# Full-array state reads, and the row of scores fetched through DRAM, in a cross-attention block followed by a mixture-of-depths layer

## The chip, the cores and the metric

One core of one Trainium2 chip. The metric is device time in microseconds of one execution; the kernel before has a median of 221.9 us over 3 runs (221.47 to 222.27). Less is better. Engines are called by their profile names: PE is TensorE's matmul, PEld its weight load, DVE VectorE, ACT ScalarE, POOL GpSimd, SP the engine whose queue issues most DMAs.

## What is computed

There are 8 batches. Each has 8 heads of 512 tokens x 64 values (x) and 8 heads of 32 state rows x 64 values (state), all f32. An attention block reads in both directions, and its 512 + 32 = 544 rows of 512 values go through a layer that only the 128 rows with the highest gate score pass:

```python
scores = scale * np.matmul(x, state.transpose(0, 1, 3, 2))      # per head 512 x 32
a = softmax over the 32 state rows;   xread = np.matmul(a, state)
scores2 = scale * np.matmul(state, x.transpose(0, 1, 3, 2))     # per head 32 x 512
a2 = softmax over the 512 tokens;     sread = np.matmul(a2, x)
x = concatenate([xread, sread]) with heads side by side         # 8 x 544 x 512
scores = np.einsum('bsd,d->bs', x, w_gate)
out = x.copy()
for b in range(B):
    top_idx = np.argpartition(-scores[b], capacity)[:capacity]  # capacity 128
    xe = x[b, top_idx]
    ye = np.maximum(xe @ w1, 0.0) @ w2                          # w1 512 x 1024, w2 1024 x 512
    out[b, top_idx] = xe + sigmoid(scores[b, top_idx])[:, None] * ye
```

## The kernel before, in words

**Attention, per batch.** Tokens are cut into NC = 4 chunks of 128 rows. The heads are turned in pairs on TensorE (L340) and copied out to xT (L349, a ring of 12 buffers). One set of small matmuls makes the scores of all heads (L369) in a PSUM tile ps_s, from which both softmaxes are made. The token side is turned 32x32 by VectorE into e (L383), then max, subtraction, exp (ACT), sum, division, and turned back into eT (L405), a chain on VectorE of some 1.2 us per step. The state side takes its max on VectorE (L411) and its exp on ACT (L415), is turned on TensorE (L469), copied to aT (L472) and multiplied with x (L485), which gives the state rows xt (L490).

**Reads.** eT holds, for a chunk c and a group g of four heads, 4 x 32 = 128 rows: one per head and state row. The reads (L447) multiply it with st_v, which holds the state rows of two heads side by side with zeros elsewhere, and as a last column each state row's product with w_gate. Each matmul takes half the array (64 rows, 129 columns out), so a chunk takes four, written to one PSUM tile ps_o of two banks (a ring of 1). ACT copies the 512 values of a row to xs (L451), and VectorE sums the gate columns (4 per row) into sc[:, b, c] (L455). When the four chunks are there, xs is stored to the output by one DMA of 1 MB on SP (L512), the state rows by four small ones (L517). GpSimd fills st_v (`pool_states`, L223): a clear (L224) and four copies (L218), for batches 0 and 1, then for 2 to 7.

**Choice, per batch.** A row's place in the order of scores is found by counting. The 544 scores of a batch are laid as a row over all partitions (srow): TensorE turns each column of sc, broadcast, into ps_tr (L558 for the tokens, L561 for the state rows) and ACT copies the two pieces (L564, L567). VectorE compares srow with each chunk's column in five win instructions (L577) that also count; TensorE sums the wins (L604); VectorE makes offsets (L610, L611) and one-hots, one instruction per chunk (L617); TensorE picks the chosen rows' numbers and scores with them (L632); VectorE makes indices (L637); GpSimd fetches the chosen rows from the output by an indirect DMA (L524), which waits for the stores of the batch.

**Layer.** Batches go in the groups 0; 1, 2; 3, 4; 5, 6; 7. The fetched rows are turned (L690), multiplied with w1 (L707, 256 columns for two batches, 128 for one), taken through ReLU by ACT (L711), multiplied with w2 (L724), added to the fetched rows by VectorE (L727) and put back by an indirect DMA (L524).

**Order.** Every step is a `Piece` with an engine, a planned length, what must come before it and the ring buffers that it takes or uses. `carry_out` (L112) makes a list plan at build time: it takes the engine that is free first, and among the pieces that are ready within SOON of that engine's free time the one with the lowest key, which is the batch's or group's number plus the number in LATER for the piece's name. The order that comes out is fixed for each engine, and each engine runs its list in order, SP's DMA issues included.

Of the kernel before, what the change touches and what calls it, by code (L numbers as in the profile page):

```python
# [8 lines left out]
F32 = mybir.dt.float32  # L9
# [9 lines left out]
def kernel(  # L19
# [10 lines left out]
    nc = tc.nc  # L30
# [24 lines left out]
    def pool(name, bufs, **kw):  # L55
        return ctx.enter_context(tc.tile_pool(name=name, bufs=bufs, **kw))

    N_X, N_XR = 5, 8
# [4 lines left out]
    psum = pool("psum", 1, space=bass.MemoryType.PSUM)  # L63

# [5 lines left out]
    SOON = {"PE": 0.0000, "DVE": 0.4931, "ACT": 0.0000, "POOL": 1.8045, "SP": 0.3000}  # L70

    LATER = {
        "add": -100.0000, "below": 1.9500, "exp": -0.0600, "exps": -0.7084, "fetch": 0.2600, "first": 100.0000,
        "gate": -0.5600, "gate_s": 4.8280, "heads": 0.4872, "in": -1.0433, "index": -2.8646, "load": -50.0000,
        "load_x": -2.0000, "max": 4.0896, "mult": 4.3959, "numbers": 0.2545, "off": -1.9260, "oh": -2.4538,
        "out": 3.4200, "over": -2.2366, "parts": -2.6851, "pick": 0.3200, "put": -100.0000, "read": 4.9387,
        "relu": -100.0000, "row": -4.7962, "row_kept": 4.8694, "row_s": -3.1695, "row_s_kept": -0.1742,
        "rows": 5.0000, "score_s": -3.7680, "scores": -1.0816, "second": 100.0000, "sexp": -0.1370,
        "sigmoid": 0.2238, "smax": 1.1888, "sread": 1.2957, "srows": -2.7199, "ssum": 1.4281, "state_T": 0.3300,
        "state_gates": 2.6509, "states": -1.3434, "store": 4.7700, "sub": -1.8119, "sum": -4.7918,  # L80
        "tables": -4.6345, "turn": -0.1899, "turn_a": 4.0218, "turned": 4.7352, "turned_a": -5.0000,
        "twice": -2.9080, "win": 4.2491, "xg": 90.0000, "xg_kept": -100.0000,
# [29 lines left out]
    def carry_out():  # L112
# [7 lines left out]
        while left:  # L120
# [15 lines left out]
            assert ready, "the plan cannot go on"  # L136
# [19 lines left out]
    P_O = Ring("ps_o", [128, 1024], F32, 1, psum)  # L156
    P_H = Ring("ps_h", [128, 512], F32, 2, psum)
    R_X = Ring("xf", [128, H, NC, D], F32, N_X, xin)
    R_XT = sbuf("xT", [128, 2, 2, 128], 12)
# [4 lines left out]
    R_XS = sbuf("xs", [128, NC, Dm], 2)  # L164
# [32 lines left out]
    st_v = const.tile([128, B, 2, 2 * D + 1], F32, name="st_v")  # L197
# [8 lines left out]
    st_T = const.tile([128, B, 2, 128], F32, name="st_T")  # L206
    z0 = const.tile([128, 1], F32, name="z0")
# [5 lines left out]
    def state_V(lo, hi):  # L213

        for q in range(4):
            k = q % 2
            r = slice(Ns * q, Ns * (q + 1))
            nc.gpsimd.tensor_copy(out=st_v[r, lo:hi, :, D * k:D * (k + 1)], in_=st_c[r, lo:hi, :, 0])  # L218
# [8 lines left out]
    def state_gates(lo, hi):  # L227
        t = work.tile([128, hi - lo, 2, D], F32, name="state_g", tag="hT", bufs=1)
        nc.vector.tensor_tensor(out=t, in0=st_c[:, lo:hi, :, 0],
                                in1=wg_s.unsqueeze(1).to_broadcast([128, hi - lo, 2, D]), op=ALU.mult)  # L230
        nc.vector.reduce_sum(out=st_v[:, lo:hi, :, 2 * D], in_=t, axis=AX.X)

    def pool_tables():

        nc.gpsimd.iota(num[:, 0, :, 0:NC], pattern=[[SP, B], [1, NC]], base=0, channel_multiplier=NC)
        nc.gpsimd.iota(num[:, 0, :, NC], pattern=[[SP, B]], base=S, channel_multiplier=1)
        nc.gpsimd.iota(after, pattern=[[1, SP]], base=0, channel_multiplier=-1, allow_small_or_imprecise_dtypes=True)
        nc.gpsimd.tensor_scalar(after, after, 0.0, None, op0=ALU.is_gt)

        nc.gpsimd.iota(places, pattern=[[-128, NC + 1], [1, n_slots]], base=0, channel_multiplier=-1,  # L240
                       allow_small_or_imprecise_dtypes=True)
        nc.gpsimd.memset(ones, 1.0)


        nc.gpsimd.memset(sc, 0.0)

# [79 lines left out]
    def attention(b):  # L326
# [6 lines left out]
        for pair in range(H // 2):  # L333
# [18 lines left out]
            p = add("PE", 0.47 if b else 0.9, turn, after=[px[(pair * len(px)) // (H // 2)]] + last_turn[-1:], takes=[ps], uses=[xf[b]],  # L352
                    key=key("turn"))
            last_turn.append(p)
            p_xT.append(add(on, 0.6, keep, after=[p], takes=[t], uses=[ps], key=key("turned")))
# [17 lines left out]
        p_s = add("PE", 1.02, scores, after=p_xT + [p_sT[b]], takes=[s], uses=xT, key=key("scores"))  # L373
# [62 lines left out]
        p_xs, p_sc = [], []  # L436
        for c in range(NC):
            o = Buf(P_O)

            def view(o):  # L440
                return o.ap.rearrange("p (i g m) -> p i g m", i=2, g=2)

            def read(c=c, o=o):
                for g in range(2):
                    for i in range(2):
                        half = slice(D * i, D * (i + 1))
                        nc.tensor.matmul(view(o)[:, i, g, 0:2 * D + 1], eT.ap[half, c % 2, g, c // 2], st_v[half, b, g],  # L447
                                         start=True, stop=True)

            def keep(c=c, o=o):  # L450
                nc.scalar.copy(out=xs.ap[:, c].rearrange("p (g i m) -> p g i m", g=2, i=2),  # L451
                               in_=view(o)[:, :, :, 0:2 * D].rearrange("p i g m -> p g i m"))

            def gate(c=c, o=o):
                nc.vector.tensor_reduce(out=sc[:, b, c:c + 1], in_=view(o)[:, :, :, 2 * D], axis=AX.XY, op=ALU.add)  # L455

            p = add("PE", 0.66, read, after=[p_eT, p_pool[b], p_sg[b]], takes=[o], uses=[eT],
                    key=key("read"))
            p_sc.append(add("DVE", 0.15, gate, after=[p, p_tab], uses=[o], key=key("gate")))
            p_xs.append(add("ACT", 0.6, keep, after=[p], takes=[] if c else [xs], uses=[o] + ([xs] if c else []), key=key("rows")))  # L460

        aT, p_aT = [], []
        for g in range(2):
# [10 lines left out]
            p = add("PE", 0.5, turn, after=[p_a[g]], takes=[ps, t], uses=[a], key=key("turn_a"))  # L474
# [35 lines left out]
    def store_base(b, xs, tmp, p_xs, p_xt):  # L510
        def x_rows():
            touches(b, nc.sync.dma_start(out=out[b, 0:S].rearrange("(p c) m -> p c m", c=NC), in_=xs.ap))  # L512
# [16 lines left out]
    def choice(b, tmp, p_sc, p_xt, p_st1):  # L529
# [30 lines left out]
        def row_s():  # L560
            nc.tensor.transpose(ps2.ap[:, 0:Ns], sc[0:Ns, b, NC:NC + 1].to_broadcast([Ns, 128]), ident[0:Ns, 0:Ns])  # L561

        p = add("PE", 0.55, row_x, after=p_sc, takes=[ps1], key=key("row"))
        p_r1 = add("ACT", 0.59, lambda: nc.scalar.copy(out=srow.ap[:, 0:S], in_=ps1.ap), after=[p], takes=[srow],  # L564
                   uses=[ps1], key=key("row_kept"))
        p = add("PE", 0.2, row_s, after=[p_ss, p], takes=[ps2], key=key("row_s"))
        p_r2 = add("ACT", 0.2, lambda: nc.scalar.copy(out=srow.ap[:, S:SP], in_=ps2.ap[:, 0:Ns]), after=[p, p_r1],  # L567
                   uses=[srow, ps2], key=key("row_s_kept"))
# [38 lines left out]
        def offsets():  # L607
            off = tmp["off"] = small.tile([128, NC + 1], F32, name="off")
# [5 lines left out]
        def one_hot():  # L614
            for c in range(NC + 1):
                m = rows[c]
                nc.vector.tensor_scalar(oh.ap[0:m, c], places[0:m, c], tmp["off"][0:m, c:c + 1], None, op0=ALU.is_equal)  # L617
# [3 lines left out]
        p_oh = add("DVE", 1.06 * n_slots / 128, one_hot, after=[p], takes=[oh], key=key("oh"))  # L621
# [169 lines left out]
```

## Time and profile before

The page comes from one profiled execution. Its own time is 222.47 us: a span of 220.7 us on the core, and 1.8 us around it. The runs without it have their median at 221.9.

| | before |
|---|---|
| median of 3 runs | 221.9 us |
| the profiled execution | 222.47 us |
| its span | 220.7 us |
| first matmul starts | 4.07 us |
| last matmul ends | 215.4 us |
| PE busy, share of the span | 202.4 us, 92% |
| DVE, ACT, POOL busy | 124.5, 85.9, 49.9 us |
| granted TensorE clock | 0.999 |
| DMA | 26.59 MB in 17,406 packets |

How to read it: a group's line has line number, engine, operation, out<-in with shapes and count, then the busy time of the group in us and the mean length of one in ns, then the idle time of the engine ahead of it with what ended it. An f32 matmul has two records, so 128 matmuls are "x256". Matmuls overlap, so lengths of single records do not add up to time; the distance from one start to the next does. The view of windows gives the busy time of each engine between two times.

### The profile page before, as it was taken

To read this page: it belongs to the slowest core of one execution; us is meant where nothing else is said; L and a number is where in the kernel's file an instruction comes from. 1 tells how busy PE (TensorE), PEld (TensorE's weight loads), DVE (VectorE), ACT (ScalarE), POOL (GpSimd) and SP (SyncE) were. 2 spreads that over 40 slices of the span, in tenths; PEclk is the share of its full clock that TensorE was granted. 3 is DMA by queue.
4 is the path that set the end of the run, shared out by engine and by line. 5 is a ranking of instruction groups with operands and counts; after the bars stand their busy time and mean duration, and the time that the engine had idled before them with its cause. 6 is when DMAs were issued, how large, how long until landed. Compare 5 with 4: busy or idle time off the path is not lost.

```text
span 220.7 us, 4784 instructions
## 1 busy us (share of the span) xinstructions
PE 202.4 (92%) x1928; PEld 142.4 (65%) x1928; DVE 124.5 (56%) x349; ACT 85.9 (39%) x172; POOL 49.9 (23%) x128
## 2 busy tenths in 40 slices
PE   2497898898999999999999999999999999999990
PEld 2355675676878954778886455888645788447840
DVE  3159989987887897798868896730062100011001
ACT  3139878778776315453725133323301021100200
POOL 7229001041105124110142423301035200011001
PEclk9999999999999999999999999999999999999999
DMA  6999969826314301150050711502212000010001
GB/s 213 329 306 402 369 207 288 305 54 205 131 74 157 111 0 48 52 196 9 34 207 13 238 50 49 239 3 95 95 48 94 33 19 0 0 50 11 36 0 48
DMA packets 17406, 26.59 MB, mean 120 GB/s; under 512 B 5608, under 2 KB 13800, under 8 KB 16360
## 3 DMA queue, kind: packets, MB, share of 16 engines
q1 hardware_dynamic: 15032, 21.43, 28.0%
q0 software_dynamic: 1280, 4.20, 6.1%
q10 hardware_dynamic: 1072, 0.66, 0.9%
q8 instruction: 15, 0.25, 0.5%
q14 instruction: 7, 0.06, 0.1%
HBM read 15.27 MB, written 11.01 MB: 119 GB/s over the span
## 4 chain that ended last, share of the span: by engine, by line
PE 55%; issue 20%; DMA 8%; POOL 6%; ACT 5%; DVE 2%; POOLq 1%; ACTq 0%
PE ps_h L707 17%; PE ps_h L724 12%; PE ps_o L447 7%; DMA out_dram<-xs 4%; PE ps_tr L340 4%; PE ps_s L369 3%; DMA xf<-in_state_dram 3%; PE ps_tr L469 3%; PE ps_tr L485 3%; ACT a L415 2%; POOL out_dram L524 2%; PE ps_tr L604 2%; PE ps_tr L558 2%; POOL xr L524 1%; ACT xT L349 1%
## 5 line engine op out<-in xcount | busy, mean ns | idle before, releaser
L707 PE MATMUL ps_h<-xg,w 128*128 128x256 f32 (+1 forms) x320 | 60.4, 341 | 0.0
L724 PE MATMUL ps_h<-w,hT 128*128 128x512 f32 x128 | 58.9, 601 | 0.0
L707 PEld LDWEIGHTS ps_h<-xg,w 128*128 128x128 f32 x320 | 50.3, 191 | 5.9 <-issue 0.5
L724 PEld LDWEIGHTS ps_h<-w,hT 128*128 128x128 f32 x128 | 23.1, 190 | 23.2 <-issue 22.5
L340 PE MATMUL ps_tr<-ident,xf 128*128 128x128 f32 x128 | 21.5, 311 | 9.7 <-DMA xf<-in_x_dram 4.1
L727 DVE SCALAR_TENSOR_TENSOR ot<-ps_h,z,xr 128x512 f32<-128x512 f32 x8 | 6.0, 749 | 43.1 <-PE ps_h L724 43.1
L451 ACT COPY xs<-ps_o 128x512 f32<-128x512 f32 x32 | 18.8, 586 | 28.2 <-PE ps_o L447 14.1
L711 ACT ACTIVATE hT<-ps_h 128x512 f32<-128x512 f32 x16 | 9.5, 596 | 49.7 <-PE ps_h L707 49.7
L340 PEld LDWEIGHTS ps_tr<-ident,xf 128*128 128x128 f32 x128 | 15.5, 156 | 14.8 <-issue 5.3
L577 DVE SCALAR_TENSOR_TENSOR win<-srow,sc,after 128x544 bf16<-128x544 f32 (+4 forms) x40 | 18.3, 501 | 8.4 <-ACT srow L567 8.4
L447 PE MATMUL ps_o<-st_v,eT 64*128 64x129 f32 x256 | 22.9, 297 | 0.1
L447 PEld LDWEIGHTS ps_o<-st_v,eT 64*128 64x128 f32 x256 | 16.8, 186 | 6.0 <-issue 2.8
L349 ACT COPY xT<-ps_tr 128x512 f32<-128x512 f32 x30 | 16.8, 589 | 9.6 <-PE ps_tr L340 9.6
L524 POOL DMA_INDIRECT out_dram<-ot,idx x8 | 8.4, 1047 | 53.2 <-DVE ot L727 51.0
L524 POOL DMA_INDIRECT xr<-out_dram,idx x8 | 8.5, 1057 | 48.1 <-DVE idx L637 16.3
L588 POOL CAST aux<-sc 128x5 bf16<-128x5 f32 x8 | 1.9, 232 | 52.3 <-DVE sc L455 38.3
L455 DVE TENSOR_REDUCE sc<-ps_o 128x1 f32<-128x4 f32 x32 | 5.1, 158 | 12.1 <-PE ps_o L447 7.0
L415 ACT ACTIVATE a<-ps_s,nm 128x512 f32<-128x512 f32 x16 | 10.9, 689 | 2.0 <-DVE nm L411 2.0
L383 DVE STREAM_TRANSPOSE e<-ps_s 128x1024 f32<-128x1024 f32 x8 | 10.0, 1247 | 2.9 <-PE ps_s L369 2.9
L369 PE MATMUL ps_s<-xT,st_T 64*32 64x256 f32 x256 | 9.6, 413 | 1.7 <-ACT a L415 1.7
L469 PE MATMUL ps_tr<-ident,a 128*128 128x128 f32 x64 | 10.2, 284 | 1.1 <-ACT a L415 0.5
L397 DVE TENSOR_REDUCE sm<-e 128x32 f32<-128x1024 f32 x8 | 9.7, 1210 | 1.5 <-ACT e L393 1.5
(84 smaller groups left out, 229.9 us busy)
## 6 DMA issues: line engine op xcount, KB each, us to landing
out_dram<-xs SPq DMA_DIRECT2D x8, 1024.0 KB, 4.3
xf<-in_x_dram SPq DMA_DIRECT2D x14, 512.0 KB, 6.8
w<-in_moe_w_dram SPq DMA_DIRECT2D x2, 2048.0 KB, 10.1
xf<-in_x_dram SPq DMA_DIRECT2D x2, 256.0 KB, 3.2
xf<-in_x_dram ACTq DMA_DIRECT2D x2, 256.0 KB
out_dram<-xt SPq DMA_DIRECT2D x32, 16.0 KB, 2.1
xf<-in_state_dram SPq DMA_DIRECT2D x1, 384.0 KB
xf<-in_state_dram ACTq DMA_DIRECT2D x1, 128.0 KB, 7.1
```

The source lines that it names most:

```text
L340: nc.tensor.transpose(v[:, k, r], xf[b].ap[:, 2 * pair + k, 2 * r:2 * r + 2].rearrange("p w d -> p (w d)"), ident)
L349: nc.scalar.copy(out=t.ap, in_=v)
L369: nc.tensor.matmul(view_s()[Ns * q:Ns * (q + 1), w, g], st_T[half, b, g, Ns * q:Ns * (q + 1)], xT[2 * g + q // 2].ap[half, q % 2].rearrang ...
L383: nc.vector.transpose(out=flat(e), in_=s.ap)
L415: nc.scalar.activation(out=a.ap[:, g], in_=view_s()[:, :, g], func=AF.Exp, bias=tmp["nm"][:, g:g + 1], accum_out=tmp["ss"][:, g:g + 1])
L447: nc.tensor.matmul(view(o)[:, i, g, 0:2 * D + 1], eT.ap[half, c % 2, g, c // 2], st_v[half, b, g], start=True, stop=True)
L451: nc.scalar.copy(out=xs.ap[:, c].rearrange("p (g i m) -> p g i m", g=2, i=2), in_=view(o)[:, :, :, 0:2 * D].rearrange("p i g m -> p g i m"))
L469: nc.tensor.transpose(v[:, c], a.ap[:, g, c % 2, 128 * (c // 2):128 * (c // 2 + 1)], ident)
L524: touches(b, nc.gpsimd.indirect_dma_start(**kw), True)
L577: nc.vector.scalar_tensor_tensor(wins[c].ap[0:n], srow.ap[0:n, f:SP], sc[0:n, b, c:c + 1], after[0:n, 0:SP - f], op0=ALU.is_gt, op1=ALU.mu ...
L707: nc.tensor.matmul(v[:, f, 0:n], w1[:, j, 128 * (f0 + f):128 * (f0 + f + 1)], xg.ap[:, j, 0:n], start=(j == 0), stop=(j == ND - 1))
L724: nc.tensor.matmul(py.ap[0:m], hT.ap[:, f, lo:lo + m], w2[:, f], start=(f == 0), stop=(f == NF - 1))
```

## The change

Three edits in the work, and what goes with them in rings and plan:

1. **Reads.** st_v gets all four heads of a group, each in its own columns (4 x 64 and the gate's column, DV = 257 in all), with zeros elsewhere. A read is then one matmul over all 128 rows with 257 columns out; a chunk takes two, each into a PSUM tile of its own (ps_o: one bank, a ring of 2). ACT copies 257 values twice per chunk, the gate's column with them; xs is stored from 1 KB pieces instead of 8 KB, and has room for the gates. One sum per batch takes the gates from xs. GpSimd clears twice as much of st_v.
2. **Row of scores.** In batches 1 to 7 two DMAs on SP store the scores to DRAM (512 from 128 partitions x 4 columns, and 32), and a third reads the 544 back into every partition of srow. Batch 0 goes on by way of TensorE and ACT.
3. **One-hots.** One tensor_tensor over 640 columns instead of five tensor_scalar; the offsets are in two fixed buffers that GpSimd clears at the start.

Rings: xT 12 to 8 buffers, and a buffer is taken when TensorE turns, not when the copy is made; xr 8 to 6. All numbers in LATER and SOON are others, and some planned lengths, so the order of work on all engines is a different one throughout. The diff, cut:

```diff
-    N_X, N_XR = 5, 8
+    N_X, N_XR = 5, 6
+    BY_DRAM = range(1, B)
+    DV = 4 * D + 1
...
-    P_O = Ring("ps_o", [128, 1024], F32, 1, psum)
+    P_O = Ring("ps_o", [128, 512], F32, 2, psum)
...
-    R_XT = sbuf("xT", [128, 2, 2, 128], 12)
+    R_XT = sbuf("xT", [128, 2, 2, 128], 8)
...
-    R_XS = sbuf("xs", [128, NC, Dm], 2)
+    R_XS = sbuf("xs", [128, NC, 2, 4 * D + 4], 2 if cap <= 128 else 1)
+    R_SD = Ring("scores_d", [SP], F32, 2, dram)
...
-            k = q % 2
             r = slice(Ns * q, Ns * (q + 1))
-            nc.gpsimd.tensor_copy(out=st_v[r, lo:hi, :, D * k:D * (k + 1)], in_=st_c[r, lo:hi, :, 0])
+            nc.gpsimd.tensor_copy(out=st_v[r, lo:hi, :, D * q:D * (q + 1)], in_=st_c[r, lo:hi, :, 0])
...
         for c in range(NC):
-            o = Buf(P_O)
...
-            def read(c=c, o=o):
-                for g in range(2):
-                    for i in range(2):
-                        half = slice(D * i, D * (i + 1))
-                        nc.tensor.matmul(view(o)[:, i, g, 0:2 * D + 1], eT.ap[half, c % 2, g, c // 2], st_v[half, b, g],
-                                         start=True, stop=True)
...
-            p = add("PE", 0.66, read, after=[p_eT, p_pool[b], p_sg[b]], takes=[o], uses=[eT],
-                    key=key("read"))
-            p_sc.append(add("DVE", 0.15, gate, after=[p, p_tab], uses=[o], key=key("gate")))
-            p_xs.append(add("ACT", 0.6, keep, after=[p], takes=[] if c else [xs], uses=[o] + ([xs] if c else []), key=key("rows")))
+            for g in range(2):
+                o = Buf(P_O)
+                def read(c=c, g=g, o=o):
+                    nc.tensor.matmul(o.ap[:, 0:DV], eT.ap[:, c % 2, g, c // 2], st_v[:, b, g], start=True, stop=True)
+                def keep(c=c, g=g, o=o):
+                    nc.scalar.copy(out=xs.ap[:, c, g, 0:DV], in_=o.ap[:, 0:DV])
+                p = add("PE", 0.22, read, after=[p_eT, p_pool[b], p_sg[b]], takes=[o], uses=[eT], key=key("read"))
+                p_xs.append(add("ACT", 0.37, keep, after=[p], takes=[xs] if not p_xs else [], uses=[o] + ([xs] if p_xs else []),
+                                key=key("rows")))
+        def gate():
+            nc.vector.reduce_sum(out=sc[:, b, 0:NC], in_=xs.ap[:, :, :, 4 * D], axis=AX.X)
+        p_sc = [add("DVE", 0.15, gate, after=p_xs + [p_tab], uses=[xs], key=key("gate"))]
...
-            touches(b, nc.sync.dma_start(out=out[b, 0:S].rearrange("(p c) m -> p c m", c=NC), in_=xs.ap))
+            touches(b, nc.sync.dma_start(out=out[b, 0:S].rearrange("(p c) (g m) -> p c g m", c=NC, g=2), in_=xs.ap[:, :, :, 0:4 * D]))
...
+        def row_out():
+            with nc.allow_non_contiguous_dma(reason="scores by place"):
+                nc.sync.dma_start(out=scores_d.ap[0:S].rearrange("(c p) -> p c", c=NC), in_=sc[:, b, 0:NC])
+                nc.sync.dma_start(out=scores_d.ap[S:SP].rearrange("(p c) -> p c", c=1), in_=sc[0:Ns, b, NC:NC + 1])
+        def row_in():
+            nc.sync.dma_start(out=srow.ap, in_=scores_d.ap.unsqueeze(0).to_broadcast([128, SP]))
+        if b in BY_DRAM:
+            p = add("SP", 1.2, row_out, after=p_sc + [p_ss], takes=[scores_d], key=key("row_out"), lands=2.0)
+            p_r1 = p_r2 = add("SP", 0.6, row_in, after=[p], takes=[srow], uses=[scores_d], key=key("row_in"), lands=2.2)
+        else:
...
         def one_hot():
-            for c in range(NC + 1):
-                m = rows[c]
-                nc.vector.tensor_scalar(oh.ap[0:m, c], places[0:m, c], tmp["off"][0:m, c:c + 1], None, op0=ALU.is_equal)
+            nc.vector.tensor_tensor(out=oh.ap, in0=places, in1=offs[b % 2].unsqueeze(2).to_broadcast([128, NC + 1, n_slots]),
+                                    op=ALU.is_equal)
```

## The prediction

> **What bounds the kernel now.** I read the busy shares and the slices first, then the windows by stage, the groups by shape, the timeline of TensorE, and last the DMA issues.
>
> ```profile
> PE 202.4 (92%) x1928; PEld 142.4 (65%) x1928; DVE 124.5 (56%) x349; ACT 85.9 (39%) x172; POOL 49.9 (23%) x128
> ```
> ```profile
> 28.00:50.00 22.00, 19.81 (x340) 15.11 (x341) 19.66 (x51) 16.30 (x34) 3.89 (x11) 1.00 0.66 212
> 50.00:60.00 10.00, 9.00 (x157) 7.25 (x156) 7.91 (x20) 8.13 (x18) 1.14 (x5) 1.00 0.49 159
> 60.00:80.00 20.00, 19.98 (x315) 16.02 (x314) 17.16 (x60) 10.10 (x21) 3.87 (x11) 1.00 0.31 108
> 80.00:91.00 11.00, 10.19 (x90) 6.29 (x89) 8.72 (x22) 5.83 (x12) 4.31 (x9) 1.00 0.16 50
> 91.00:216.00 125.00, 124.37 (x821) 84.25 (x819) 54.10 (x176) 30.50 (x60) 23.12 (x67) 1.00 0.19 67
> ```
> The columns of the windows are length, then busy time of PE, PEld, DVE, ACT, POOL, the granted clock, the DMA share and GB/s. Up to 91 us TensorE idles a little (2.2, 1.0, 0.0 and 0.8 us), while VectorE is nearly as full as it is. From 91 us on TensorE never waits (its last matmul ends at 215.4). So a microsecond of TensorE work after 91 us is a microsecond of the kernel, time on the other engines is worth nothing there unless TensorE comes to wait for it, and before 91 us at most 4.0 us of idle time can be closed.
>
> The lines of the part that changes, by shape:
> ```profile
> L447 PE MATMUL ps_o<-st_v,eT 64*128 64x129 f32 x256 | 22.9, 297 | 0.1
> L451 ACT COPY xs<-ps_o 128x512 f32<-128x512 f32 x32 | 18.8, 586 | 28.2 <-PE ps_o L447 14.1 <-DVE sc L455 13.7 <-DVE rs L420 0.3
> L455 DVE TENSOR_REDUCE sc<-ps_o 128x1 f32<-128x4 f32 x32 | 5.1, 158 | 12.1 <-PE ps_o L447 7.0 <-ACT xs L451 4.9
> L617 DVE TENSOR_SCALAR oh<-places,off 128x128 bf16<-128x128 f32 x32 | 7.0, 282 | 0.0
> ```
> A mean of a pipelined matmul is no price, so I price by start to next start, in the timeline of TensorE (start, length, what; two records for each f32 matmul):
> ```profile
> 137.79 1.99 PE L707 MATMUL ps_h<-xg,w 128*128 128x256 f32 x8
> 139.62 0.60 PE L558 MATMUL ps_tr<-ident,sc 128*128 128x128 f32 x4
> 140.16 0.24 PE L561 MATMUL ps_tr<-ident,sc 32*128 32x32 f32 x1
> 140.32 1.99 PE L707 MATMUL ps_h<-xg,w 128*128 128x256 f32 x8
> ...
> 145.72 0.72 PE L447 MATMUL ps_o<-st_v,eT 64*128 64x129 f32 x8
> 146.37 1.99 PE L707 MATMUL ps_h<-xg,w 128*128 128x256 f32 x8
> 148.29 0.72 PE L447 MATMUL ps_o<-st_v,eT 64*128 64x129 f32 x8
> 148.94 1.99 PE L707 MATMUL ps_h<-xg,w 128*128 128x256 f32 x8
> 150.86 0.72 PE L447 MATMUL ps_o<-st_v,eT 64*128 64x129 f32 x8
> ```
> One group of reads takes 146.37 - 145.72 = 0.65 us. The 64 records of L707 that run in one piece (173.69 to 187.50) give 0.216 us a record, 1.73 for eight; from 146.37 to 148.29 eight take 1.92, so 0.19 more is lost where the array goes over from a full-array matmul to half-array reads.
>
> [...] at 0.216 us x 129/256 a record their eight would take 0.87 us one after the other, and take 0.65. [...]
>
> **The change, part by part.**
>
> *Reads (TensorE).* 128 matmuls of 129 columns on 64 rows become 64 of 257 columns on 128 rows. This is the shape of L707 (128x128 weights, 256 columns): 2 x 0.216 x 257/256 = 0.433 us each, 0.867 for the two of a chunk, against 0.65. Over 32 chunks that is +6.9. Eight groups follow L707 or L724 directly and lose their 0.19, -1.5. Sum +5.4. The new plan counts 0.22 us for such a read, half of what L707 shows; the plan sets only the order.
>
> *Row of scores (TensorE).* L558 and L561 go in seven batches: 139.62 to 140.32 is 0.70, and the eight records of L707 before it take 1.83 instead of 1.73, 0.10 more. 7 x 0.80 = -5.6. So TensorE's work changes by -0.2: it gives for wider reads what it gets for the row.
>
> *ACT.* Copies of 512 and 32 elements take 587 and 193 ns (L564, L567), so 257 take about 0.38: eight make 3.0 us per batch where four made 2.3; the two row copies, 0.78, go. Nothing in sum; the copies no longer take turns with VectorE over one double bank, since the gate now comes from xs.
>
> *VectorE.* Four gate sums of 0.16 become one, -0.4 per batch with their waits' hops; the five one-hots (1.06 in the timeline) become one tensor_tensor of 640 elements. L390 (1024 elements) takes 1.21 and L490 (128) 0.27, so 640 take about 0.81: -0.25. Eight batches: -5 us of VectorE, worth nothing after 91 us.
>
> *GpSimd.* The clears of st_v double (0.52 and 1.39 us); the second state copy ends near 23.4 instead of 22.0. The first read needs eT at 27.2 anyway: nothing. If GpSimd were 4 us later the reads would wait. The two new off buffers are cleared before.
>
> *Rings.* xT goes from 12 to 8 buffers, so transposes run two batches ahead, not three; xr from 8 to 6. TensorE has other work in its order in both cases: nothing by itself, up to 1 us before 60 us if not.
>
> *Order in the first part.* In the built order the first two reads now stand ahead of L485 of batch 0 and of the scores of batch 2, and wait there for eT (27.2), while the transposes before them end near 26.1: +1.1 of idle. From there VectorE's chain for batch 2 runs about 1 us late, and the win sums of batch 0 find TensorE waiting near 43 to 45 us, where before it lost some 1.9 us in pieces behind xT copies. SP now puts the small stores of batches 0 and 1 and the 1 MB of batch 0 ahead of the last loads of x; walking the order with the durations above, the half of x[5] that is behind them comes about when TensorE asks for it (near 48 us). I take +0.7 for the first part: from -2 (VectorE's relief) to +4 (late x).
>
> *The way by DRAM.* Each of seven batches adds three DMAs on SP: two stores (544 runs of 4 bytes) and a read back into 128 partitions of 2,176 bytes. SP waits for the stores before it issues the read; behind it in SP's queue stand the small stores of a later batch and the next 1 MB, which no engine needs soon except through the fetch (L524), some 10 us away. VectorE's win instructions wait for the read, and behind them softmax work of later batches; TensorE's win sums wait for those.
> ```profile
> out_dram<-xs SPq DMA_DIRECT2D x8, 1024.0 KB, 4.3
> xf<-in_x_dram SPq DMA_DIRECT2D x14, 512.0 KB, 6.8
> out_dram<-xt SPq DMA_DIRECT2D x32, 16.0 KB, 2.1
> ```
> A small store lands in 2.1 us and costs SP 0.57 to issue. Low end of the trip: 1.2 (two issues) + 2.1 + 0.5 + 2.1 = 5.9. High end: SP's queue took 28.0% of 16 engines for 15,032 packets, 66 ns each; 34 tiny packets per engine make 2.2 more; in batches 1, 2, 4, 6 and 7 the 1 MB store of the same batch is issued between the scores' stores and the read, and if it is drained first: 1.5 + 2.2 + 4.3 + 2.1 = 10.1. I take 1.5 + 1.1 + (4.3 - 2.1) + 0.5 + 2.1 = 7.4; in batches 3 and 5 the 1 MB goes ahead of the scores too, 9.4 (12 at the high end). To it come the last ACT copy 0.4, the gate 0.3 and the five win instructions 2.2: 10.3 and 12.3 us from the last read to the win sums.
>
> What TensorE has in between, summed from the built order at the prices above: batch 1 10.9 us, 2 11.3, 3 15, 4 12.4, 5 11.0, 6 14.4, 7 10.1. So batch 7 waits 0.2 us, batch 5 1.3, and about 1 more, because its last read's copy stands behind an exponential that waits for GpSimd. Sum +2.5 (0 to 11.5 between the bounds: 2.0, 1.6, 0.5, 4.6 and 2.8 for batches 1, 2, 4, 5 and 7).
>
> **Sum.** 222.47 (the profiled execution, of which 220.7 is span; the last 5 us after TensorE stay) - 0.2 + 0.7 + 2.5 = 225.5. The profiled execution lies 0.57 over the median of 221.9, so 224.9 on the scale of the median.
>
> **The rivals.**
> *Slow trips.* 66 ns for each 4-byte packet and the 1 MB store drained first: with trips of about 9 and 11 us batches 1, 2, 5 and 7 wait 1.0, 0.6, 3.6 and 1.8, 7 in all instead of 2.5, with the late first part 230. For it: 1 MB every time near the read. Against: no 4-byte run measured.
> *Faster.* VectorE decides below 91 us: its 0.65 us less per batch and the two single PSUM banks close half of the 4.0 us of idle, and no trip is waited for (it must stay below about 7.2 us, for batch 7): 222.47 - 0.2 - 2.0 - 0.57 = 219.7. For it: DVE at 19.66 of 22. Against: the wait put ahead of L485.
> *Hidden.* Trips hidden, first part unchanged: about 221.9.
> *Not what L707 shows.* The reads take the plan's 0.22: 64 x 0.22 = 14.1 instead of 27.7, so 225.5 - 13.6, about 211. Against: 64 records of the same shape at 0.216.
>
> **How the numbers follow.** Forecast 0.43, slow trips 0.22, faster 0.19, hidden 0.13, the plan's price 0.03. Measurement can tell about 0.3% (0.7 us) from no change. Faster: 0.19 + 0.03 + 0.02 of the hidden case; same: the rest of it, 0.11, and 0.02 of the forecast; slower: the rest, 0.63. The range goes from the faster case's 219.7 to just over the slow trips' 230; likeliest alone, 223 to 227.5.
>
> **What would show it.** Reads at 0.43 a matmul and full-array groups without the 0.19 after L707; no L558 after batch 0; TensorE busy within 2 us of 202.4; idle of TensorE before the win sums of batches 5 and 7 with VectorE's win, and behind it the read back, as the releaser; 1 us idle before the first read. I am wrong if the reads are cheaper than 0.4 us, if no win waits for the read back, or if TensorE waits before 91 us for something else.

## The result, and the profile after

The changed kernel takes 288.4 us (median of 4 runs, 287.3 to 291.6) where the kernel before takes 222.1 in the same session (median of 4, 221.5 to 223.4): a ratio of 1.296, 95% interval 1.286 to 1.306. The forecast was 224.9, and its range ended just over 230. Runs more than 1.5% above the fastest of their kernel do not enter the ratios, here and below, and the profiled execution is one of them (291.6 us at a clock of 0.878, the other three at 0.893 to 0.900), so its microseconds lie about 1% above those of the median.

Its page, the busy shares and the clock by slices (each digit of PEclk is tenths of full speed):
```profile
PE 222.6 (77%) x1765; PEld 157.4 (54%) x1765; DVE 121.3 (42%) x293; ACT 85.4 (29%) x190; POOL 50.2 (17%) x130
...
PEclk9799999977995999779589995599596599999998
```
The span is 289.9 us instead of 220.7, +69.2. TensorE is busy 20.2 us longer, though by the prices of the prediction it has no more to do, and is idle 67.3 us instead of 18.3, +49.0. The clock was 0.999 on average before; here it falls to 5 to 7 tenths again and again. The windows by stage, to be set beside those of before (length, busy time of PE, PEld, DVE, ACT, POOL, then clock, DMA share, GB/s):
```profile
60.00:80.00 20.00, 15.16 (x135) 12.93 (x136) 10.21 (x28) 7.30 (x15) 3.23 (x9) 0.83 0.62 68
80.00:91.00 11.00, 5.09 (x85) 4.48 (x84) 2.51 (x9) 2.56 (x7) 1.16 (x2) 0.77 0.79 116
91.00:216.00 125.00, 96.88 (x672) 70.30 (x671) 57.02 (x146) 31.82 (x76) 17.96 (x54) 0.84 0.43 63
```
TensorE did not wait after 91 us before; now it is busy for 97 of 125 us. The DMA share in the last window has gone from 0.19 to 0.43 while fewer GB/s are moved (63 instead of 67). This is not the small stores themselves: in the packet records of the trace the 4-byte packets are marked with some 8 ns each, 2.6 us in all as a mean of the 16 engines. What has grown is the time of the other packets: the 15,872 of 1,024 bytes on SP's queue take 95 us per engine, more than all packets of that queue in e1 below (29.0% of 229.0 us, 66 us): the other transfers take longer. What TensorE and VectorE wait for, from the view of waits (us in total, times, longest):
```profile
DVE win L594 <- DMA srow<-scores_d: 48.1, 7, 14.9
PE ps_tr L487 <- issue: 24.7, 8, 6.7
PE ps_tr L621 <- DVE win L594: 17.7, 6, 8.9
PE ps_tr L706 <- DMA xr<-out_dram,idx: 5.5, 1, 5.5
```
The last three make 47.9 of the 49.0 us of new idle time. None of them is in the list of the kernel before, which goes down to 0.2 us. Only the 17.7 are the wait that the prediction looked for: TensorE's win sums behind VectorE's wins behind the row. The 24.7 have no releaser that the profile shows ("issue"): TensorE stops inside the 64 records of the matmuls that make the state rows (L487, before L485; called state-row matmuls below, and state reads in the expectations), after it has begun on the same operands.

The DMA issues (KB each, median us from issue to landing), against 4.3 us for the 1 MB store before:
```profile
out_dram<-xs SPq DMA_DIRECT2D x8, 1024.0 KB, 12.6
srow<-scores_d SPq DMA_DIRECT2D x7, 272.0 KB, 3.6
scores_d<-sc SPq DMA_DIRECT2D x7, 0.1 KB, 13.5
```
SP's timeline around batch 2's row (start, length of the issue, what):
```profile
75.47 0.37 SPq L570 DMA_DIRECT2D scores_d<-sc  x1
75.89 0.50 SPq L571 DMA_DIRECT2D scores_d<-sc  x1
76.49 0.58 SPq L514 DMA_DIRECT2D out_dram<-xs  x1
87.17 0.33 SPq L574 DMA_DIRECT2D srow<-scores_d  x1
```
The read back (L574) waits until both score stores (L570, L571) have landed: 11.7 us after the first was issued; over the seven batches 11.5 to 14.7. (The 13.5 us of the list are of the few 32-run stores whose landing the profile caught; by SP's timeline the read back comes 11.1 to 14.0 us after their issue.) TensorE early on (first line), and in the microseconds of batch 2's row:
```profile
25.07 1.18 PE L471 MATMUL ps_tr<-ident,a 128*128 128x128 f32 x8 [0.21 <-ACT xT L357]
...
81.31 0.74 PE L487 MATMUL ps_tr<-xf,aT 128*32 128x64 f32 x34
87.49 0.27 PE L487 MATMUL ps_tr<-xf,aT 128*32 128x64 f32 x1 [5.43 <-issue]
88.23 1.10 PE L487 MATMUL ps_tr<-xf,aT 128*32 128x64 f32 x29 [0.47 <-issue]
89.27 1.97 PE L471 MATMUL ps_tr<-ident,a 128*128 128x128 f32 x8
```
It does 34 of the 64 records, stops for 5.43 us, and goes on at 87.49, about when the stores are through (87.17; in batches 1 and 4 it goes on 0.7 and 0.5 us before that). Eight records of L471 then take 1.97 us where eight took 1.18 at full clock. Later, after the next stop, eight records of L723 take 2.94 us from start to next start (124.48 to 127.42), against 1.73 for those of L707 before. The granted clock in the view of windows is 0.50 from 88 to 92 us and from 121 to 126.

What the prediction priced on the engines themselves came as priced. By shape:
```profile
L450 PE MATMUL ps_o<-st_v,eT 128*128 128x257 f32 x128 | 38.0, 416 | 0.3 <-DVE eT L413 0.3
L632 DVE TENSOR_TENSOR oh<-places,off 128x640 bf16<-128x640 f32 x8 | 6.6, 824 | 0.2
```
The reads' pipelined mean of 416 ns holds stretches of low clock; start to start, four records (two reads) go from 31.99 to 32.86 us in the timeline, 0.435 us a read.

### The profile page after: what moved, and what is told of

Same layout as the page of the kernel before. It is cut to its first block, busy times and chain, and to the rows that moved or that the text cites. A ratio compares the mean times of both kernels' runs of the same rounds, so it can differ in the third digit from the quotient of the medians.

```text
span 289.9 us, 4454 instructions
## 1 busy us (share of the span) xinstructions
PE 222.6 (77%) x1765; PEld 157.4 (54%) x1765; DVE 121.3 (42%) x293; ACT 85.4 (29%) x190; POOL 50.2 (17%) x130
## 4 chain that ended last, share of the span: by engine, by line
PE 40%; issue 26%; DMA 19%; DVE 8%; ACT 2%; POOL 2%; SPq 1%; POOLq 0%; ACTq 0%
DMA scores_d<-sc 13%; PE ps_o L450 10%; PE ps_h L723 9%; PE ps_h L740 6%; PE ps_tr L487 4%; DMA srow<-scores_d 4%; PE ps_tr L348 3%; PE ps_tr L471 3%; DMA xf<-in_state_dram 3%; PE ps_s L377 2%; DVE win L594 2%; POOL out_dram L526 1%; PE ps_tr L621 1%; ACT xT L357 1%; DVE nm L419 1%
## 5 line engine op out<-in xcount | busy, mean ns | idle before, releaser
L723 PE MATMUL ps_h<-xg,w 128*128 128x256 f32 (+1 forms) x320 | 66.3, 364 | 0.0
L723 PEld LDWEIGHTS ps_h<-xg,w 128*128 128x128 f32 x320 | 56.6, 210 | 7.9 <-issue 1.4
L453 ACT COPY xs<-ps_o 128x257 f32<-128x257 f32 x64 | 23.6, 377 | 54.6 <-PE ps_o L450 53.7
L740 PEld LDWEIGHTS ps_h<-w,hT 128*128 128x128 f32 x128 | 25.3, 203 | 25.4 <-issue 24.7
L594 DVE SCALAR_TENSOR_TENSOR win<-srow,sc,after 128x544 bf16<-128x544 f32 (+4 forms) x40 | 18.3, 513 | 48.1 <-DMA srow<-scores_d 48.1
L450 PE MATMUL ps_o<-st_v,eT 128*128 128x257 f32 x128 | 38.0, 416 | 0.3 <-DVE eT L413 0.3
L487 PE MATMUL ps_tr<-xf,aT 128*32 128x64 f32 x512 | 12.8, 231 | 25.2 <-issue 24.7
L450 PEld LDWEIGHTS ps_o<-st_v,eT 128*128 128x128 f32 x128 | 23.7, 202 | 7.4 <-issue 3.7
L487 PEld LDWEIGHTS ps_tr<-xf,aT 128*32 128x32 f32 x512 | 9.7, 115 | 28.1 <-issue 26.4
L621 PE MATMUL ps_tr<-ones,win 128*128 128x1 bf16 (+2 forms) x120 | 6.5, 167 | 17.8 <-DVE win L594 17.7
L357 ACT COPY xT<-ps_tr 128x512 f32<-128x512 f32 x30 | 16.8, 587 | 10.3 <-PE ps_tr L348 10.3
L621 PEld LDWEIGHTS <-win 128*128 128x128 bf16 (+2 forms) x120 | 5.5, 98 | 19.6 <-DVE win L594 18.5
L492 DVE TENSOR_TENSOR xt<-ps_tr,rs 128x128 f32<-128x128 f32 x8 | 2.3, 292 | 32.6 <-PE ps_tr L487 24.7
L474 ACT COPY aT<-ps_tr 128x512 f32<-128x512 f32 x16 | 9.3, 584 | 12.4 <-PE ps_tr L471 12.0
## 6 DMA issues: line engine op xcount, KB each, us to landing
out_dram<-xs SPq DMA_DIRECT2D x8, 1024.0 KB, 12.6
```

The lines of the kernel that those rows point to most:

```text
L357: nc.scalar.copy(out=t.ap, in_=v)
L450: nc.tensor.matmul(o.ap[:, 0:DV], eT.ap[:, c % 2, g, c // 2], st_v[:, b, g], start=True, stop=True)
L453: nc.scalar.copy(out=xs.ap[:, c, g, 0:DV], in_=o.ap[:, 0:DV])
L474: nc.scalar.copy(out=t.ap, in_=ps.ap.rearrange("p (c m) -> p c m", c=NC))
L487: nc.tensor.matmul(o2.ap[rr, D * g:D * (g + 1)], aT[g].ap[:, c, rr], xf[b].ap[:, 4 * g + q, c], start=(c == 0), stop=(c == NC - 1))
L594: nc.vector.scalar_tensor_tensor(wins[c].ap[0:n], srow.ap[0:n, f:SP], sc[0:n, b, c:c + 1], after[0:n, 0:SP - f], op0=ALU.is_gt, op1=ALU.mu ...
```

## The experiments

The theory after the first look, A: a store in runs of 4 bytes (a run is a contiguous piece of a transfer) to DRAM takes the DMA engines for some 10 us. That holds up the row, but also everything else that goes through the engines, the 1 MB store (12.6 us instead of 4.3), the fetch and, by the author's guess, TensorE; and after a stop TensorE works at a lower clock for a while (0.50 from 88 to 92 us, after the stop of 5.43 us). The main rivals: B, the reads and the new order are the cause; C, only the waiting for the row (theory D in e3's text); D, the long landing comes from the 1 MB store beside (theory C in e2's text, for its 1 KB runs). The kernel before took 222.6 us beside e1 to e4, 223.2 beside e6 and e7, 222.8 beside e8 to e11 and 222.5 beside e12.

**e1_pe_rows**: the changed kernel with the row on TensorE in all batches.
```diff
-    BY_DRAM = range(1, B)
+    BY_DRAM = range(0)
```


> The changed kernel with the row of scores made on TensorE in all eight batches; reads, one-hots, rings and plan numbers as changed. Theory A (the 4-byte stores keep the 16 DMA engines busy for some 11 us a batch, and all that needs these engines[...] waits): no stall of L487 or of the win sums, time about 228: 225.5 less the 2.5 of waits, plus 5.6 for the row on TensorE, less 0.6 for the median. Theory B (the wide reads or the new order cost the time): well over 240.

Measured: 230.6 us, ratio 1.036 (1.031 to 1.041). Span 229.0, TensorE busy 208.0, clock 0.995; the state-row matmuls never stop, the 1 MB store lands in 5.2 us. So 58 of the 66 us come with the row's way by DRAM, and B falls for the bulk; A's 228 was 2.6 too low (see e8 and e10).

**e2_before_dram**: the kernel before with the row's way by DRAM as its only edit, reads and all else as before.
```diff
+    BY_DRAM = range(1, B)
...
-        p = add("PE", 0.55, row_x, after=p_sc, takes=[ps1], key=key("row"))
+        if b in BY_DRAM:
+            p = add("SP", 1.2, row_out, after=p_sc + [p_ss], takes=[scores_d], key=key("row_out"), lands=2.0)
+            p_r1 = p_r2 = add("SP", 0.6, row_in, after=[p], takes=[srow], uses=[scores_d], key=key("row_in"), lands=2.2)
```


> The kernel before with only the row of batches 1 to 7 by way of DRAM; reads and one-hots as before. Theory A: most of the loss comes with it, 265 to 285, the stores land 10 to 12 us after issue though the 1 MB store still has runs of 8 KB. Theory B: 222 to 230. Theory C (it is the 1 MB store in 1 KB runs that holds up the row): the row's trip is 6 to 8 us and the time under 235.

Measured: 290.9 us, ratio 1.305 (1.300 to 1.309). More than the upper end of A's range, and as much as the whole loss from this one edit. The read back is issued 9.4 to 13.5 us after the first store, though the 1 MB store has its runs of 8 KB here, and none is issued between the stores and the read back: theory C of the text above falls. The one landing of a store of 512 runs that the view gives is 10.6 us.
```profile
DVE win L594 <- DMA srow<-scores_d: 75.7, 7, 16.7
PE ps_tr L488 <- issue: 5.4, 4, 2.6
```
So the same loss is made up differently here. TensorE is idle 70.5 us, 52.2 more than before, and 41.6 us of its waits are for VectorE's wins, a pick and gate sums, and for copies of ACT; the longest of them end just after a VectorE that stood for the row goes on. Stops without a releaser are only 5.4.

**e3_idle_4b**: e1, and the score stores are issued as well, in the same places, but nobody reads them: the row comes by TensorE, and TensorE's order is e1's.
```diff
+            if b:
+                add("SP", 1.2, row_out, after=p_sc + [p_ss], takes=[scores_d], key=key("row_out"), lands=2.0)
             p = add("PE", 0.62, row_x, after=p_sc, takes=[ps1], key=key("row"))
```


> The row on TensorE in all batches, and in batches 1 to 7 the two score stores are issued besides; nobody reads what they store. Theory A: TensorE still stops in the middle of L487 or other runs of short matmuls for some 5 us per batch, 245 to 275, although no instruction waits for the stores' data. Theory D (the whole loss is the wait of the win instructions for the row): about 228, as without the stores.

Measured: 259.5 us, ratio 1.166 (1.159 to 1.173), clock 0.947. Stores whose data nobody waits for cost 28.9 us over e1 on the same chip, half of the 58. TensorE's waits that e1 hardly had:
```profile
PE ps_tr L708 <- DMA xr<-out_dram,idx: 9.9, 3, 4.0
PE ps_tr L487 <- issue: 4.6, 2, 3.5
```
The fetch of the chosen rows (landing 8.1 us instead of 3.6) and again the state-row matmuls that stop without a releaser. Of the 28.5 us by which the span grows, 17.0 are idle and 11.5 are busy time of the same instructions: the clock. C falls: the wait for the row is only part of it. A gave the size, but not the make-up: it had stops of some 5 us per batch, and they are 4.6 us in all; the fetch makes more.

**e4_idle_16b**: e3 with the same bytes in 128 runs of 16 bytes (the order of the scores in DRAM is another, nobody reads them; the 32 scores of the state rows stay single).
```diff
-                nc.sync.dma_start(out=scores_d.ap[0:S].rearrange("(c p) -> p c", c=NC), in_=sc[:, b, 0:NC])
+                nc.sync.dma_start(out=scores_d.ap[0:S].rearrange("(p c) -> p c", c=NC), in_=sc[:, b, 0:NC])
```


> As the run with idle stores, but the 512 scores are stored as 128 runs of 16 bytes instead of 512 of 4, the same bytes (nobody reads them; the 32 of the state rows stay single). Theory A, the cost goes by the number of runs: 10 instead of 34 per DMA engine, landing after 4 to 5 us, stalls of TensorE 0 to 1 us a batch, 228 to 234. If the cost is that of a store from the gate sums' tile or of DRAM whatever the runs: as the run with 4-byte runs.

Measured: 233.0 us, ratio 1.045 (1.041 to 1.049): 2.4 over e1 instead of 28.9. The store lands in 4.4 us (2.1 to 7.1), the 1 MB in 7.2, and no stop in the state-row matmuls. Bytes and DMAs are as many as in e3; fewer and longer runs take nearly all of the loss away.

**e5_micro**: the stores by themselves; the computation is left out. One DMA after another on SP, then small and wide matmuls beside 4-byte stores, and the same with quiet queues. `st4` stores 512 values in runs of 4 bytes, `st16` in runs of 16, `back` reads them back, `ld4` reads runs of 4 bytes from DRAM into SBUF.
```diff
+    for i in range(2):
+        st4()
+        back(d4)
+    for i in range(2):
+        st16()
+        back(d16)
...
+    ld4()
...
+    for i in range(6):
+        st4()
+        back(d4)
+    wide(24)
+    narrow(120)
+    wide(12)
...
+    wide(30)
+    narrow(120)
+    wide(12)
```


> A measurement by itself, which leaves the whole computation out. First, with nothing else running, 512 values are written to DRAM from 128 partitions and read back: as 512 runs of 4 bytes, as 128 runs of 16 bytes, as 4 runs of 512 bytes, each twice, then 4-byte runs are read from DRAM. Then six more stores of 4-byte runs with their read back, while TensorE does 24 wide matmuls (512 columns), 480 small ones (64 columns on a quarter of the array's columns, as in the state reads), 12 wide; then the same with the DMA queues quiet. Theory A (a run costs 0.27 to 0.33 us on its DMA engine [...], 32 runs per engine): 4-byte stores 10 to 12 us, 16-byte stores 2 + 8 x 0.3 = 4.5, 512-byte stores 2 to 2.5; the small matmuls stop for microseconds during the stores, [...] the wide ones hardly, and neither in the quiet part. Rival D (the long stores in the kernel come from the 1 MB transfers beside them, and a 4-byte run alone costs what its packet costs, 66 ns): 4-byte stores alone 4 to 5 us, and no stop of TensorE's small matmuls.

Measured, SP's timeline; of each pair, the second is issued when the first has landed (L57 is the store of 4-byte runs, L66 the read back, L70 the 4-byte read from DRAM):
```profile
19.75 0.37 SPq L57 DMA_DIRECT2D d<-sc  x1
27.77 0.32 SPq L66 DMA_DIRECT2D srow<-d  x1
...
46.66 0.44 SPq L70 DMA_DIRECT2D sc<-d  x1
49.73 0.37 SPq L57 DMA_DIRECT2D d<-sc  x1
```
With no other DMA of the kernel beside it, a store of 512 runs of 4 bytes takes 8.0 us from issue to the next step (all 9 such stores, six of them beside matmuls: 8.1 to 10.3 to landing, median 8.3), 128 runs of 16 bytes 2.6 and 4.7, 4 runs of 512 bytes at most 2.8. Reading 512 runs of 4 bytes from DRAM takes 3.1. So it is the writing to DRAM; D falls, as the time is there without the 1 MB. A's 10 to 12 was too high for a store that has the engines for itself. As an estimate, (8.3 - 2.8) / 512 runs is 11 ns a run, or 0.17 us if each of 16 engines does every 16th; the one 10.6 of e2 less 2.1, the shortest store of 128 runs (in e4), gives 0.27 for 32 runs on an engine, with other transfers beside.

TensorE in the same kernel. The first three lines are beside stores, the last two with quiet queues:
```profile
64.30 26.70 PE L87 MATMUL ps_w<-xw 128*128 128x512 f32 x60
...
112.04 1.99 PE L92 MATMUL ps_n<-xs,xw 128*32 128x64 f32 x128 [2.87 <-issue]
117.14 4.77 PE L92 MATMUL ps_n<-xs,xw 128*32 128x64 f32 x205 [3.11 <-issue]
...
144.04 27.61 PE L87 MATMUL ps_w<-xw 128*128 128x512 f32 x60
...
179.99 1.99 PE L92 MATMUL ps_n<-xs,xw 128*32 128x64 f32 x128 [1.46 <-issue]
```
The 60 records of wide matmuls run through in both. The 960 records of small ones take 37.3 us (90.92 to 128.26) beside stores and 24.5 (171.58 to 196.11) without. When quiet they come mostly in pieces of 128 with pauses of 1.0 to 2.0 us, where the expectation had none; beside stores the pauses are mostly 2.3 to 3.8. The profile shows no releaser for these pauses ("issue"). The DMA view has a queue of the kind "instruction" beside SP's: 7 packets, 0.11 MB in the window from 90 to 128 us, 16 KB each, each taking some 2.3 us of one engine (2.6% of 16 engines in 38 us); 1.1 us when quiet (8 packets, 0.9% in 62 us). So its packets, too, take longer beside the stores; that the pauses wait for them was not shown. The stops of the changed kernel are up to 6.7 us, longer than any here. Its DMA view has no packet of that queue from 54 to 66, from 75 to 89 and from 129 to 142 us, around the three longest stops, so no late packet is seen to end them. What TensorE waits for there stays open; that the stops come with the stores and go without them is shown by e1, e4 and e6.

**e6_after_512b**: the changed kernel, scores turned on TensorE to 5 x 128 first, so that the store has 5 runs of 512 bytes.
```diff
+        def row_turn():
+            nc.tensor.transpose(ps1.ap[0:NC + 1, 0:128], sc[:, b], ident)
...
         def row_out():
...
-                nc.sync.dma_start(out=scores_d.ap[0:S].rearrange("(c p) -> p c", c=NC), in_=sc[:, b, 0:NC])
-                nc.sync.dma_start(out=scores_d.ap[S:SP].rearrange("(p c) -> p c", c=1), in_=sc[0:Ns, b, NC:NC + 1])
+            nc.sync.dma_start(out=scores_d.ap.rearrange("(c p) -> c p", p=128), in_=sc_r.ap)
```


> The changed kernel, with the scores turned on TensorE from 128 x 5 to 5 x 128 (one small transpose and one copy on ACT per batch), so that the store to DRAM has 5 runs of 512 bytes instead of 544 of 4; reads and read back as in the changed kernel. Theory A (the 4-byte runs are the cause): e1's 230.6 less 5.6 for the row on TensorE, plus 7 x 0.2 for the turns, about 226.5, 223 to 231, TensorE busy about 204, no stop inside the state reads, clock over 0.99. Rival E (a trip through DRAM in this place is too long for what TensorE has in between, whatever its runs): over 240, with waits for the win instructions of several us in most batches.

Measured: 230.8 us, ratio 1.037 (1.029 to 1.046); clock 0.998, the waits for wins sum to 0.7 us, 0.2 us of stops in the state-row matmuls. The way by DRAM with long runs, on the same path with the same read back, costs none of the 58 us. It brings nothing over e1 either: TensorE is busy 206.3 instead of 208.0, and idle 1.2 us more. The 226.5 that A named were missed, within its range to 231.

**e7_before_512b**: the same way by DRAM on the kernel before (half-array reads). The edit is that of e2 with e6's `row_turn` and `row_out`.

> The kernel before with half-array reads, and the row of scores of batches 1 to 7 by way of DRAM in 5 runs of 512 bytes, turned on TensorE by one small transpose. Theory A: 222.6 - 5.6 + 1.4 = 218.4, plus 0 to 3 for waits for the trip: 218 to 222. Rival E (trip too long in any form): over 235.

Measured: 224.9 us, ratio 1.011 (1.001 to 1.020). Not the gain that was expected. TensorE is busy 200.2 instead of 202.4, but it waits 1.2 us for a fetch and 0.7 for the copy behind it, in the stretch around 91 us, and the clock is 0.985 on average: eight records of L731 take 3.46 us to the next start in that stretch (92.78 to 96.24), against 1.92 later (100.60 to 102.52).

**e8_before_wide**: the kernel before with the first edit alone (st_v, reads, ps_o, xs, the gate; 6 xr buffers for room).
```diff
-    P_O = Ring("ps_o", [128, 1024], F32, 1, psum)
+    P_O = Ring("ps_o", [128, 512], F32, 2, psum)
...
-                        nc.tensor.matmul(view(o)[:, i, g, 0:2 * D + 1], eT.ap[half, c % 2, g, c // 2], st_v[half, b, g],
-                                         start=True, stop=True)
+                    nc.tensor.matmul(o.ap[:, 0:DV], eT.ap[:, c % 2, g, c // 2], st_v[:, b, g], start=True, stop=True)
```


> The kernel before with the first edit alone: full-array reads by halves (st_v, ps_o, xs and the gate's sum with them) and 6 xr buffers for room; row on TensorE, one-hots, xT ring and all numbers of the plan as in the kernel before. My step on the reads (+5.4 on TensorE, 0.433 us a matmul): TensorE busy 207.8, and 228 us if nothing else comes of it. Rival F (the +7.9 of e1 is the reads alone: the copies and the gate that now waits for all eight of them cost another 2.5): 230 to 231.

Measured: 228.0 us, ratio 1.024 (1.018 to 1.030), TensorE busy 208.7, clock 1.00: 5.1 over the kernel before. The reads cost what their step said; F falls.

**e10_after_half**: e1 with the half-array reads.
```diff
-    P_O = Ring("ps_o", [128, 512], F32, 2, psum)
+    P_O = Ring("ps_o", [128, 1024], F32, 1, psum)
...
-                p = add("PE", 0.22, read, after=[p_eT, p_pool[b], p_sg[b]], takes=[o], uses=[eT], key=key("read"))
+            p = add("PE", 0.66, read, after=[p_eT, p_pool[b], p_sg[b]], takes=[o], uses=[eT],
+                    key=key("read"))
```


> e1 (the changed kernel with the row on TensorE) with the half-array reads of the kernel before: what is left of the change is the one-hots, the xT ring of 8 taken at the turn, and the numbers of the plan. My step (0.7 us late first part, TensorE's work as before): 223.3. Rival G (plan and rings cost the 2.5 us that e1 has over the reads' price): 225 to 226. Rival F: 222 to 223.

Measured: 236.8 us, ratio 1.054 (1.045 to 1.063), which is none of the three expectations. The plan makes another order of the same pieces: in the profiled execution (238.9 us) TensorE waits 3.6 us, up to 45.7, for a load of x, and the clock is 0.84 and 0.68 in the windows 28 to 50 and 50 to 60 us; all four runs have a clock of 0.957 to 0.970. So the new numbers of the plan cannot be told from the reads in this way. What e1 has over e8 (1.036 against 1.024, some 2.5 us) fits e1's idle time, 21.0 us instead of 18.3, but which number or ring makes it stays open.

**e11_before_onehot**: the kernel before with the third edit alone.
```diff
-            for c in range(NC + 1):
-                m = rows[c]
-                nc.vector.tensor_scalar(oh.ap[0:m, c], places[0:m, c], tmp["off"][0:m, c:c + 1], None, op0=ALU.is_equal)
+            nc.vector.tensor_tensor(out=oh.ap, in0=places, in1=offs[b % 2].unsqueeze(2).to_broadcast([128, NC + 1, n_slots]),
+                                    op=ALU.is_equal)
```


> The kernel before with the third edit alone: one tensor_tensor of 640 elements instead of five one-hots. My step: 0.25 us of VectorE per batch, nothing for the time: within 0.7 us of the kernel before.

Measured: 222.4 us over 12 runs, ratio 1.000 (0.997 to 1.002). Nothing, as said.

**e9_after_sbuf**: the changed kernel with the 4-byte runs gathered into one partition of SBUF, and one run of 2,176 bytes from there to DRAM.
```diff
+        def row_flat():
+            with nc.allow_non_contiguous_dma(reason="scores by place"):
+                for c in range(NC):
+                    nc.sync.dma_start(out=sc_1.ap[:, 128 * c:128 * (c + 1)], in_=sc[:, b, c:c + 1])
+                nc.sync.dma_start(out=sc_1.ap[:, S:SP], in_=sc[0:Ns, b, NC:NC + 1])
+
         def row_out():
-                nc.sync.dma_start(out=scores_d.ap[0:S].rearrange("(c p) -> p c", c=NC), in_=sc[:, b, 0:NC])
-                nc.sync.dma_start(out=scores_d.ap[S:SP].rearrange("(p c) -> p c", c=1), in_=sc[0:Ns, b, NC:NC + 1])
+            nc.sync.dma_start(out=scores_d.ap.unsqueeze(0), in_=sc_1.ap)
```


> The changed kernel with the scores gathered by 4-byte runs into one partition of SBUF (five DMAs), stored from there to DRAM as one run of 2176 bytes, and read back as in the changed kernel: 544 runs of 4 bytes as before, but none is written to DRAM. Theory A1 (the 4-byte WRITE TO DRAM is what is dear; a read of 512 runs of 4 bytes from DRAM to SBUF came back in 3.1 us by itself, a store of them in 8 to 10): a trip of 3 + 2 + 3.5 = 8.5 us and its issues, engines not clogged: 228 to 238. Theory A2 (every 4-byte run costs 0.3 us wherever it lands): 285 or more.

Measured: 239.4 us, ratio 1.074 (1.066 to 1.081), just above A1's range and far from A2's. 128 runs of 4 bytes into SBUF land in 2.0 us, the 1 MB store in 5.5, and the state-row matmuls do not stop. The same 544 runs of 4 bytes, not written to DRAM, cost 49 us less in all, though three transfers now follow one another. By what mechanism the write to DRAM is dear, no trace here shows, nor whether it is the number of the runs, their shortness, or that they lie side by side in DRAM.

**e12_before_512b_due**: e7 with the trip's length told to the plan.
```diff
-            p = add("SP", 0.6, row_out, after=[p], takes=[scores_d], uses=[sc_r], key=key("row_out"), lands=2.0)
-            p_r1 = p_r2 = add("SP", 0.6, row_in, after=[p], takes=[srow], uses=[scores_d], key=key("row_in"), lands=2.2)
+            p = add("SP", 0.6, row_out, after=[p], takes=[scores_d], uses=[sc_r], key=key("row_out"), lands=3.3)
+            p_r1 = p_r2 = add("SP", 0.6, row_in, after=[p], takes=[srow], uses=[scores_d], key=key("row_in"), lands=3.3)
```


> e7 (half-array reads, row by way of DRAM in 5 runs of 512 bytes) with one thing in the plan changed: store and read back are planned to land 3.3 us after their issue (e7's profile shows 3.7 and 3.5 from issue to landing, read back 3.5 to 3.9) instead of 2.0 and 2.2, so the work that needs the row is put later in the orders. If e7's 2 us over the kernel before come from orders that expect the row too early: 219 to 222. If TensorE's saving of some 4 us is lost to something else (a lower clock after the first waits, the late fetch), still 223 to 226.

Measured: 222.8 us over 18 runs (219.9 to 225.1) beside 222.5 over 23; the ratio, without eight of the 18, is 0.997 (0.994 to 1.001): not to be told from the kernel before. It lies between the two expectations. Its profiled execution, one of the shortest, has a span of 218.5 us with TensorE busy 197.2, 5.2 less than before, and idle 21.3, 3.0 more. No version that beats both kernels beyond doubt came out of the study.

## Why the prediction was wrong, step by step

*Reads, +5.4 on TensorE.* Right: 0.435 us a read against 0.433, and e8 is 5.1 us slower than the kernel before.

*Row removed, -5.6 of TensorE's work.* Not refuted, and not to be had: e12's TensorE has 5.2 us less to do (its seven small turns included), e6's only 1.7 less than e1's, and in neither does the time gain more than the measurement can tell. In the changed kernel itself TensorE is busy 222.6 us, not 202.4, mostly because of the clock: e6, with seven small turns more and a clock of 0.998, is busy 206.3.

*ACT, VectorE, GpSimd.* Right: a copy of 257 takes 377 ns (0.38 estimated), the one-hot 824 (0.81), and e11 shows that the one-hots are worth nothing.

*First part, +0.7.* Its bounds hold (-2 to +4), the value was low: e1 has 2.7 us more idle time than the kernel before. The wait of 1.1 us ahead of the first read did not come: it is 0.29 us in the changed kernel and 0.46 in e1.

*The way by DRAM.* Here the prediction failed, in two terms. The first is the trip's length, "I take 1.5 + 1.1 + (4.3 - 2.1) + 0.5 + 2.1 = 7.4", with 2.2 us as the most for the tiny packets, from 66 ns a packet. The mean of packets of 1.4 KB (21.4 MB in 15,032 packets) was taken as a ceiling for 4-byte ones. The stores alone take 8.3 us by themselves; up to the read back it is 9.4 to 13.5 in e2 and 11.5 to 14.7 in the changed kernel, with 3.0 to 4.6 more for the read: 14.5 us and more, past the upper ends of 10.1 and 12. TensorE's wait for the wins is 17.7 us instead of 2.5.

The second is what was not in the sum, a term put at nothing: that the stores hold up everything else. The sentence "behind it in SP's queue stand the small stores of a later batch and the next 1 MB, which no engine needs soon except through the fetch (L524), some 10 us away" looked at the order of SP's queue, and left out that the transfers themselves take longer, those of other queues too. e3 prices it at 28.9 us with no wait for the row in it: the fetch, which is on GpSimd's queue, lands after 8.1 us instead of 3.6, and TensorE stops in the state-row matmuls (4.6 us there, 24.7 in the changed kernel). What TensorE then does it does at a lower clock: most of the 20.2 us of new busy time in the changed kernel. The clock is 0.50 from 88 to 92 us, after the stop of 5.43 us. It falls in the quiet part of e5 too, where no pause is over 2.0 us: it is 0.86 on average from 171.5 to 196.1 us, and 5 tenths in the slice of PEclk from 190.9 to 196.2 us. What length of stop lowers it was not shown.

*The rivals.* "Slow trips" had the right place and sign; its 230 had the same ceiling in it, and its sum is not right either: 7 us of waits instead of 2.5 make 229.4, and with the late first part (+4 instead of +0.7) 232.7. The prediction said itself that no 4-byte run was measured, and then a price from another kind of packet was put in. A cost that no row shows has no upper bound until a reason gives one; here the range needed one from the 544 runs, and had none.

## What to carry to other kernels

Count the runs of a DMA, not its bytes, where it writes to DRAM: e4 moves the same bytes in 128 longer runs for 2.4 us in place of 28.9, and e6 goes by DRAM in 5 runs of 512 bytes with no loss over e1. A transfer's price is also what it does to all the others (the fetch of rows landed after 8.1 us instead of 3.6), so an experiment that issues it without a reader (e3) tells contention from waiting. How the loss is shared between the two depends on the order of the work: e2 loses as much as the changed kernel, most of it by waiting. And a saving on the busiest engine is only as good as the order that can use it: 5 us of TensorE's work less (e12) were worth no measurable time.

## What the runs showed of the hardware that was not expected

A store of 512 runs of 4 bytes to DRAM takes 8.3 us alone (median of nine in e5), a read of such runs 3.1 us (one, in e5), and a store of 128 of them into SBUF 2.0 us beside other work (e9). TensorE can stop where the profile shows nothing that it waits for: in e5, 128 records of small f32 matmuls with their loads last 1.99 us, and the next ones come 1.0 to 2.0 us later in quiet, mostly 2.3 to 3.8 us later beside such stores. And the DMA share can hide such stores: in e5 it is 13% in the window from 90.9 to 128.2 us, in which they follow each other with only a read back between them, and in the changed kernel such packets are marked with some 8 ns each. The landing times tell what the share does not.
